# One kernel for attention and two MoE blocks: the last product takes hi and lo of its weight in one matmul, its pages come in the order of use, and early scores run on pieces of the array

## The chip, the core and the metric

The kernel runs on one core of one Trainium2 chip. The metric is the device time of one execution in microseconds (us). The kernel before was run three times: 1394.1, 1395.72 and 1396.98 us, median 1395.72. Its profiled execution took 1396.56 us, with a span of 1394.8 us from the first to the last instruction; 1.76 us lie around the span. The granted TensorE clock was 0.991 of full speed on average.

## The reference

Three stages, all in float32 outside (the weights come as float64 words and are converted on the chip):

```
# attention, 8 batches, 8 heads, 512 tokens x, 32 states, 64 columns a head
a  = softmax(x @ state.T / 8);  xread = a  @ state
a2 = softmax(state @ x.T / 8);  sread = a2 @ x
x  = concat(xread, sread)                     # 8 * 544 = 4352 rows of 512
x  = relu(x @ w_in) ** 2 @ w_out              # moe,  512 -> 2048 -> 512
h  = x @ w3                                   # moe2, 512 -> 2048
out = (h * sigmoid(h)) @ w4                   # moe2, 2048 -> 512
```

## The kernel before

**Precision.** TensorE works on two rounded parts. A float32 page of 128 partitions x 1024 is split into `hi` (a rounded copy made by ScalarE, `split_into`, line 457) and `lo` (the rest, a subtraction on VectorE or GpSimd). A product x times w is then three matmuls: hi.hi, hi.lo, lo.hi, all accumulated in one PSUM bank.

**Stages in order of time.** (1) 0 to some 50 us: the float64 words of the first weights are converted on VectorE and ScalarE, `g_unit` multiplies states by the first weight on 64x64 pieces of the array (four at once, plain float32), and the scores of batches 0 to 2 are made. (2) Up to some 850 us: the first MoE block, `gemm1`, `chain_a`, `gemm2`. (3) Some 850 to 1030 us: `gemm3`, the first product of the second block, in Strassen-Winograd form: 7 products of half matrices (numbers 1 to 7) whose sums give the four quarters. Its results go to DRAM as `t`. (4) Some 1030 to 1390 us: `gemm4(q)`, the second product in the same form, q = 0 to 8 (q = 8 has half the rows). The products come in the order 1, 6, 2, 7, 5, 4, 3 (`SEQ4`).

**gemm4.** Each product i of a q needs two half pages from DRAM, `g<q><i>0` and `g<q><i>1` (0.5 MB each), each split into hi and lo, so four pages; and four weight pages `w4<jj>_<i>`, which stay for all q, 28 in all, split when q is 0. A weight page holds for each of two row blocks 256 columns of hi and, right beside them, 256 columns of lo. The loop at lines 1051 to 1059 runs, for both halves b of the rows and 8 blocks k, three matmuls of 256 columns. Both b go into one PSUM bank of 512 columns; the four names bA to bD stand for banks that alternate with q. ScalarE copies the first product out (`u`), VectorE adds the others from PSUM into `u` or `z`, and `z[1]` (after product 4) and `z[0]` (after product 3, the last) are stored.

**What sets the order.** Nothing is ordered by hand: `Plan` records every operation with its tiles, and a list scheduler with estimated costs (`cost`, line 107) and due times writes each engine's queue. All pages come from one pool of 50; a load can be issued once its page is free. All DMAs are issued from one queue, SP's, in order. TensorE's queue often alternates between two products.

**Transition.** In the last unit of `gemm3` (u = 4), `w4_load(pp)` brings all seven pages of column block jj = pp before `gemm3(u, pp)`, for pp = 0 to 3. The pages of product 1 are therefore complete only with pp = 3.

**Scores of batches 0 to 2.** For each batch b and half g, `scores` (line 648) runs two float32 matmuls on the whole array: the stationary side is `sblkf[b]`, a 128x512 tile that is zero but for blocks of the states (set by `memset` on GpSimd, filled by `s_put`). The result psD is copied (`Sc`) and transposed by VectorE (`U`); from it the softmax on VectorE gives `AThi` and `ATlo`, on which `gemm1` starts.

Of the kernel before, what the change touches and what calls it, by code (L numbers as in the profile page):

```python
# [27 lines left out]
class Plan:  # L28
# [78 lines left out]
    def cost(self, eng, method, writes, reads, args):  # L107
        size = 1
        for ap in writes + reads:
            n = 1  # L110
            for d in ap.shape[1:]:
                n *= d
            size = max(size, n)
        psum = any(self.tiles.get(ap.tensor.name, (0, 0, ""))[2] == "ps" for ap in writes + reads)
        if eng == "dma":
            n = 1
            for d in writes[0].shape:
                n *= d
            return n * 4 / 360
        if eng == "pe":  # L120
            n = 1
            for d in writes[0].shape[1:]:
                n *= d
            if method == "transpose":
                return 109
            share = 4 if args.get("tile_position") else 1
            return max(n / 2.4 + 13, 109) * (4 if args["rhs"].dtype == F32 else 1) / share
        if eng == "act":
            return (145 if psum else 190) + size / 1.2 + (93 if "accum_out" in args else 0)
        if eng == "pool":  # L130
            return 190 + dict(tensor_tensor=2.2, memset=0.8).get(method, 3.5) * size
        fast = method in ("tensor_scalar", "tensor_copy", "memset") and not psum
        return 157 + size / (1.92 if fast else 0.96)
# [243 lines left out]
def attn_moe_moe_kernel(  # L377
# [76 lines left out]
    def copy(o, a):  # L454
        plan.either((A, "copy", dict(out=o, in_=a)), (V, "tensor_copy", dict(out=o, in_=a)))
# [101 lines left out]

    st = plan.tile(pages, [P, 4, 4, 2, NS], F32, "page", "st")
    sblk = [page(f"sblk{i}") for i in range(2)]
    sblkf = [quad(f"sblkf{b}") for b in range(NB)]  # L560
    ident = plan.tile(const, [P, P], F32, "ident", "ident")
    srT = plan.tile(pages, [P, 4, B * NS], F32, "page", "srT")

    def st_of(b, r):
        return st[r * 64:(r + 1) * 64, b // 2, :, b % 2].rearrange("p (g l) n -> p g l n", l=2)

    def s_build(b, dst, a):

        v = dst.rearrange("p (s g a c) -> p s g a c", s=2, g=2, a=4)
        for r in range(2):  # L570
# [1 line left out]
            src = st_of(b, r)  # L572
            hi, lo = (v[ps, s][:, :, a, r * NS:(r + 1) * NS] for s in range(2))
            split_into(hi, lo, src)

    def s_put(b, dst, a):

        v = dst.rearrange("p (g a c) -> p g a c", g=2, a=4)
        for r in range(2):
            ps = slice(r * 64, (r + 1) * 64)  # L580
            copy(v[ps, :, a, r * NS:(r + 1) * NS], st_of(b, r))


    w1p, gp = {}, {}
# [63 lines left out]
    def scores(b, g):  # L648
        x = a_x.pop((b, g))
        t = att_tile()  # L650
        a_S[(b, g)] = t
        if b < NB:
            for l in range(2):
                c0 = (2 * g + l) * P
                T.matmul(out=t, lhsT=sblkf[b][:, c0:c0 + P], rhs=x[:, l * 512:(l + 1) * 512],
                         start=l == 0, stop=l == 1)
            return
        hi, lo = x
        pg = sblk[b % 2]
# [265 lines left out]
    def w4_views(pg):  # L925
        v = pg.rearrange("p (k s c) -> p s k c", s=2, k=2)
        return v[:, 0], v[:, 1]

    def w4_load(jj):

        w4p[jj] = {}
        for i in SEQ4:
            w4p[jj][i] = page(f"w4{jj}_{i}")
            lo = f32(w4_views(w4p[jj][i])[1])
            if SRC_B[i] in (11, 12, 21, 22):
                w4_quarter(jj, SRC_B[i], lo)
            else:
                D.dma_start(lo, w4s_d[(SRC_B[i], jj)].rearrange("p (k c) -> p k c", k=2))

    def w4_split(jj, i):  # L940
        hi, lo = w4_views(w4p[jj][i])
        split_into(hi, lo, f32(lo))

    def x_op(u, i):
# [96 lines left out]

    def gemm4(q):

        c = 2 if q < B else 1
        n = c * 256

        def prod(i, bank, first, last):
            if q == 0:
                for jj in range(4):
                    w4_split(jj, i)  # L1050
            for b in range(c):
                for k in range(8):
                    hi, lo = gop[(q, i)][k // 4]
                    w = w4p[k // 2][i][:, k % 2 * 512:(k % 2 + 1) * 512]
                    ks = slice(k % 4 * c * P + b * P, k % 4 * c * P + (b + 1) * P)
                    for m, (g, o) in enumerate(((hi, 0), (hi, 256), (lo, 0))):
                        T.matmul(out=bank[:, b * 256:(b + 1) * 256], lhsT=g[:, ks], rhs=w[:, o:o + 256],
                                 start=first and b + k + m == 0, stop=last and k == 7 and m == 2,
                                 skip_group_check=True)

        def part(t):
            return t[:, :n].rearrange("p (b d) -> p b d", b=c)

        def add(o, bank, a):
            V.tensor_tensor(out=o, in0=part(bank), in1=a, op=ALU.add)
# [10 lines left out]
        bA, bB, bC, bD = (t[q % 2] for t in (BA, BB, BC, BD))  # L1076
        z = [page(f"z{t}", F32)[:, :c * 512].rearrange("p (b d) -> p b d", b=c) for t in range(2)]
        ls, hs = slice(0, 256), slice(256, 512)
        prod(1, bA, True, False)
        u = page("u4", F32)  # L1080
        U, W = (part(u[:, i * 512:(i + 1) * 512]) for i in range(2))
        A.copy(U, part(bA))
        prod(6, bB, True, True)
        add(U, bB, U)
        prod(2, bA, False, True)
        A.copy(z[0][:, :, ls], part(bA))
        prod(7, bD, True, False)
        add(W, bD, U)
        prod(5, bC, True, False)
        add(z[1][:, :, hs], bC, W)  # L1090
        prod(4, bD, False, True)
        add(z[1][:, :, ls], bD, U)
        store(1, z[1])
        prod(3, bC, False, True)
        add(z[0][:, :, hs], bC, U)
        store(0, z[0])


# [2 lines left out]
    def sched_attention(b, g, s, defer=False):  # L1101
        at(s - 4, "dma", x_load, b, g)
        if b >= NB:
            if g == 0:
                at(s, "vec", sblk_build, b)
            at(s, "vec", x_split, b, g)
        elif g == 0:
            at(s, "vec", s_put, b, sblkf[b], slice(0, 4, 3))
# [15 lines left out]
        at(s + 2, "vec", sread_evac, b, g)  # L1124

    def init():
        for t in sblkf:
            G.memset(t, 0.0)
        for t in sblk[::-1]:
            G.memset(t.bitcast(F32), 0.0)  # L1130

# [13 lines left out]
    for i in range(NC // 2):  # L1145
# [11 lines left out]
            at(-12, "dma", load_st)  # L1157
        at(n, "pe", g_unit, 2 * i)
        at(n, "pe", g_unit, 2 * i + 1)
    at(-10, "vec", s_put, 0, sblkf[0], slice(0, 4, 3))  # L1160
    for g in range(2):
        at(-8 + g, "dma", x_load, 0, g)
        at(-6 + g, "pe", scores, 0, g)
# [75 lines left out]
    for u in range(NU):  # L1239
        for pp in range(4):  # L1240
            plan.slot = base + 16 * u + 4 * pp
            if u == 0 and pp in (0, 1):
                w3_build(pp + 2)
            if u == 1:
                w4_sums(pp)
            if u + 1 == NU:
                if pp == 3:
                    g_op(0, 1)
                w4_load(pp)
            gemm3(u, pp)  # L1250
            if pp == 3:
                for i in (SEQ if u + 1 < NU else SEQ4[1:]):
                    if u + 1 < NU:
                        x_op(u + 1, i)
                    else:
                        g_op(0, i)
# [42 lines left out]
```

## Time and profile before

| what | value |
|---|---|
| median of three runs | 1395.72 us |
| profiled execution | 1396.56 us |
| its span | 1394.8 us |
| PE busy | 1350.0 us (97%) |
| VectorE (DVE) busy | 1006.7 us (72%) |
| ScalarE (ACT) busy | 693.0 us (50%) |
| GpSimd (POOL) busy | 44.8 us |
| DMA | 283 MB, mean 203 GB/s |

PE is TensorE's matmuls, PEld its weight loads, which run beside them. "PEclk" is the granted clock as a share of 2.4 GHz; the other level is 0.50. "DMA share" is the mean busy share of the core's 16 DMA engines. A float32 matmul that is not rounded shows as two instructions. In the rows below, `<-` after an idle time names what ended it.

### The profile page before, as it was taken

How to read it: one execution, taken by the hardware profiler on the slowest of the kernel's cores; microseconds unless marked ns; L12 is line 12 of the kernel's file. 1: busy time of each engine (PE TensorE's matmuls, PEld its weight loads, DVE VectorE, ACT ScalarE, POOL GpSimd, SP SyncE). 2: the span in 40 equal slices, each digit the busy share in tenths (PEclk: the TensorE clock that was granted, in tenths of full speed). 3: DMA queues.
4: the chain of work that ended last, by engine and by line, in shares of the span. 5: the costliest groups of instructions: out<-in, count | busy, mean ns of one | idle time of the engine just before them, and what ended most of it. 6: DMA issues, size and time to landing. Idle time of an engine off the chain costs nothing. (4 is left out here: it accounts for less than half of the span.)

```text
span 1394.8 us, 21037 instructions
## 1 busy us (share of the span) xinstructions
PE 1350.0 (97%) x7820; PEld 1169.2 (84%) x7820; DVE 1006.7 (72%) x1524; ACT 693.0 (50%) x1070; POOL 44.8 (3%) x42
## 2 busy tenths in 40 slices
PE   5889999999999999999999999999999999999998
PEld 1557688888888888888988889998879999999998
DVE  7898598878888888885997768677876455444443
ACT  6765776556555555554743424245563343333331
POOL 1000001100000000000020000000010000000000
PEclk9999999999999999999999999999999999999999
DMA  8841844535454535452759758678897566655664
GB/s 308 313 178 63 296 155 129 165 122 166 152 168 125 176 118 162 138 191 73 256 190 355 276 209 285 216 242 295 303 345 242 197 212 227 209 178 188 196 189 113
DMA packets 206965, 283.19 MB, mean 203 GB/s; under 512 B 13456, under 2 KB 148112, under 8 KB 206864
## 3 DMA queue, kind: packets, MB, share of 16 engines
q1 hardware_dynamic: 206864, 281.86, 60.7%
q8 instruction: 61, 1.00, 0.3%
q14 instruction: 40, 0.33, 0.1%
HBM read 161.35 MB, written 116.26 MB: 199 GB/s over the span
## 5 line engine op out<-in xcount | busy, mean ns | idle before, releaser
L185 ACT ACTIVATE rg<-psC 128x512 f32<-128x512 f32 (+1 forms) x144 | 82.6, 574 | 197.4 <-PE psC L185 195.4
L185 DVE TENSOR_TENSOR gact<-rg,gact 128x512 fp32r<-128x512 f32 (+1 forms) x139 | 90.8, 655 | 20.4 <-ACT rg L185 14.6
L185 PE MATMUL psC<-AThi,Ghi 128*128 128x512 f32 x256 | 100.9, 400 | 2.3 <-ACT rg L185 2.0
L185 PE MATMUL psC<-AThi,Glo 128*128 128x512 f32 x256 | 101.2, 401 | 1.6 <-DVE Glo L185 1.6
L185 PE MATMUL psC<-ATlo,Ghi 128*128 128x512 f32 x256 | 100.5, 397 | 1.9 <-DVE ATlo L185 1.9
L185 ACT ACTIVATE gact<-rg 128x512 fp32r<-128x512 f32 (+1 forms) x144 | 87.7, 609 | 7.6 <-DMA g<-go 4.1
L185 DVE TENSOR_TENSOR rg<-rg 128x512 f32<-128x512 f32 (+1 forms) x66 | 43.7, 662 | 50.5 <-ACT rg L185 50.3
L185 PEld LDWEIGHTS psC<-AThi,Ghi 128*128 128x128 f32 x256 | 48.1, 188 | 15.7 <-ACT rg L185 2.4
L185 PEld LDWEIGHTS psC<-AThi,Glo 128*128 128x128 f32 x256 | 48.2, 188 | 14.6 <-issue 2.1
L185 PEld LDWEIGHTS psC<-ATlo,Ghi 128*128 128x128 f32 x256 | 48.3, 189 | 13.8 <-DVE ATlo L185 2.6
L185 ACT ACTIVATE r<-r 128x1024 f32<-128x1024 f32 (+2 forms) x20 | 18.6, 932 | 62.9 <-DVE r L185 52.7
L185 DVE TENSOR_SCALAR cv<-cv 128x1024 f32<-128x1024 f32 (+1 forms) x64 | 43.3, 685 | 8.0 <-ACT cv L185 7.7
L185 ACT ACTIVATE rg<-rg 128x512 f32<-128x512 f32 (+1 forms) x78 | 46.3, 594 | 0.0
L185 ACT ACTIVATE cv<-raw 128x512 f32<-128x512 f32 x64 | 40.6, 667 | 7.3 <-DMA raw<-in_w_dram 6.3
L185 DVE SCALAR_TENSOR_TENSOR cc<-raw,cv 128x512 int32<-128x512 int32 x64 | 41.8, 683 | 3.3 <-DMA g<-go 3.1
L185 DVE SCALAR_TENSOR_TENSOR cv<-raw,cv 128x512 f32<-128x512 uint32 x64 | 41.6, 683 | 0.2
L185 DVE TENSOR_TENSOR W<-psC,U 128x512 f32<-128x512 f32 (+2 forms) x40 | 24.1, 609 | 22.5 <-PE psC L185 22.2
L185 PE MATMUL psA<-cc,st 64*64 64x512 f32 x128 | 26.1, 687 | 14.6 <-DVE cc L185 14.6
L185 DVE TENSOR_TENSOR Glo<-Glo,Ghi 128x1024 fp32r<-128x1024 f32 x31 | 37.7, 1215 | 1.2 <-ACT Ghi L185 1.0
L185 ACT ACTIVATE W<-W 128x1024 f32<-128x1024 f32 (+2 forms) x20 | 18.7, 933 | 39.6 <-DVE W L185 35.7
L185 ACT ACTIVATE r<-psA 128x512 f32<-128x512 f32 (+2 forms) x40 | 20.7, 534 | 33.3 <-PE psA L185 25.6
L185 ACT CAST Ghi<-Glo 128x1024 fp32r<-128x1024 f32 x32 | 33.5, 1045 | 1.2 <-DMA Glo<-go 1.2
(1244 smaller groups left out, 4587.2 us busy)
## 6 DMA issues: line engine op xcount, KB each, us to landing
raw<-in_w_dram SPq DMA_DIRECT2D x64, 512.0 KB, 6.2
t<-s SPq DMA_DIRECT2D x36, 512.0 KB, 5.1
Glo<-g SPq DMA_DIRECT2D x96, 128.0 KB, 4.3
t<-r SPq DMA_DIRECT2D x24, 512.0 KB, 4.5
xTr<-in_xT_dram SPq DMA_DIRECT2D x16, 512.0 KB, 7.6
g<-go SPq DMA_DIRECT2D x16, 512.0 KB, 5.2
xnr<-in_xN_dram SPq DMA_DIRECT2D x16, 512.0 KB, 5.2
x<-yt SPq DMA_DIRECT2D x32, 256.0 KB, 4.1
```

The source lines that it names most:

```text
L185: lambda engine=engine, method=method, a=a, k=k: getattr(engine, method)(*a, **k)))
```

## The change

Three edits.

1. `gemm4`: for each half b and block k there are two matmuls in place of three. hi.(hi and lo) is one matmul of 512 columns (the weight's hi and lo lie side by side), lo.hi one of 256 columns into the first half of the same bank. Each half b has a bank of its own (BA[0], BA[1], ...), so the banks no longer alternate with q. The two halves of a bank are now summed outside: every evacuation takes 512 columns for each b into pages of its own (`U4`, `R4`, `W4`, `X4`), and a `join` on VectorE or GpSimd adds the halves into `z`.
2. `w4_load(i, jj)` brings one page; the 28 come in the order of `SEQ4`, four for each product, seven after each `gemm3(u, pp)`.
3. `scores` for batches 0 to 2: four float32 matmuls on pieces of 64 rows x 32 columns, straight from `st`; `sblkf`, its memsets and `s_put` go. The planner's cost of a matmul on pieces goes by the size of the piece.

```diff
         if b < NB:
             for l in range(2):
-                c0 = (2 * g + l) * P
-                T.matmul(out=t, lhsT=sblkf[b][:, c0:c0 + P], rhs=x[:, l * 512:(l + 1) * 512],
-                         start=l == 0, stop=l == 1)
+                for r in range(2):
+                    h, ps = 2 * l + r, slice(r * 64, (r + 1) * 64)
+                    T.matmul(out=t[h * NS:(h + 1) * NS], lhsT=st[ps, b // 2, 2 * g + l, b % 2],
+                             rhs=x[ps, l * 512:(l + 1) * 512], start=True, stop=True, tile_position=(r * 64, h * NS))
...
-                    for m, (g, o) in enumerate(((hi, 0), (hi, 256), (lo, 0))):
-                        T.matmul(out=bank[:, b * 256:(b + 1) * 256], lhsT=g[:, ks], rhs=w[:, o:o + 256],
-                                 start=first and b + k + m == 0, stop=last and k == 7 and m == 2,
-                                 skip_group_check=True)
...
+                    T.matmul(out=banks[b], lhsT=hi[:, ks], rhs=w,
+                             start=first and k == 0, stop=False, skip_group_check=True)
+                    T.matmul(out=banks[b][:, 0:256], lhsT=lo[:, ks], rhs=w[:, 0:256],
+                             start=False, stop=last and k == 7, skip_group_check=True)
+
+        def new(name):
+            return page(name, F32)[:, :c * 512].rearrange("p (b n) -> p b n", b=c)
+
+        def add(o, banks, a):
+            for b in range(c):
+                V.tensor_tensor(out=o[:, b], in0=banks[b], in1=a[:, b], op=ALU.add)
+
+        def join(z, a):
+            arith(ALU.add, z, a[:, :, 0:256], a[:, :, 256:512])
...
+        prod(4, BD, False, True)
+        X = new("X4")
+        add(X, BD, U)
+        join(z[1][:, :, ls], X)
         store(1, z[1])
-        prod(3, bC, False, True)
-        add(z[0][:, :, hs], bC, U)
+        prod(3, BC, False, True)
+        add(U, BC, U)
+        join(z[0][:, :, hs], U)
         store(0, z[0])
...
-                w4_load(pp)
-            gemm3(u, pp)
+            gemm3(u, pp)
             if u + 1 == NU:
+                for i, jj in [(i, jj) for i in SEQ4 for jj in range(4)][7 * pp:7 * pp + 7]:
+                    w4_load(i, jj)
```

**TensorE in gemm4.** Where product 6 of q = 4 runs beside product 1; psA and psB are banks, w_1 and w_6 weight pages, g410 and g460 half pages of the stationary side (hi or lo). Before:

```order
L185 MATMUL psB_216<-w_6_1309,g460hi 128x256
L185 MATMUL psA_214<-w_1_1308,g410lo 128x256
L185 MATMUL psB_216<-w_6_1309,g460hi 128x256
L185 MATMUL psA_214<-w_1_1322,g410hi 128x256
L185 MATMUL psB_216<-w_6_1309,g460lo 128x256
L185 MATMUL psA_214<-w_1_1322,g410hi 128x256
L185 MATMUL psB_216<-w_6_1309,g460hi 128x256
```

Now:

```order
L186 MATMUL psB_216<-w_6_1316,g460hi 128x512
L186 MATMUL psA_215<-w_1_1312,g410lo 128x256
L186 MATMUL psB_216<-w_6_1316,g460lo 128x256
L186 MATMUL psA_215<-w_1_1313,g410hi 128x512
L186 MATMUL psB_216<-w_6_1316,g460hi 128x512
L186 MATMUL psA_215<-w_1_1313,g410lo 128x256
L186 MATMUL psB_216<-w_6_1316,g460lo 128x256
```

All matmuls were alike; now two long ones alternate with two short ones, and the two halves b (psA_214, psA_215) stand in banks of their own.

**VectorE in the transition.** The last sums of `gemm3` (s_ pages, stored to t) between the splits of g. With what each waits for: DVE, PE and Activation are engines, DMAHW a landing. Before:

```order
L185 TENSOR_TENSOR g020lo<-g020lo,g020hi 128x1024 [waits DMAHW1_49,Activation_49]
L185 TENSOR_TENSOR W<-r_1362,W 128x1024 [waits DVE_49]
L185 TENSOR_TENSOR s_1366<-s_1365,r_1362 128x1024 [waits PE_49]
L185 TENSOR_TENSOR g021lo<-g021lo,g021hi 128x1024 [waits DMAHW2_49,Activation_49]
L185 TENSOR_TENSOR s_1367<-U,s_1366 128x1024 [waits DMAHW0_49,DVE_49]
L185 TENSOR_TENSOR g070lo<-g070lo,g070hi 128x1024 [waits DMAHW4_49,Activation_49]
```

Now:

```order
L186 TENSOR_TENSOR W<-r_1352,W 128x1024 [waits DVE_49]
L186 TENSOR_TENSOR s_1356<-s_1355,r_1352 128x1024 [waits DMAHW0_49]
L186 TENSOR_TENSOR g020lo<-g020lo,g020hi 128x1024 [waits DMAHW1_49,Activation_49]
L186 TENSOR_TENSOR s_1357<-U,s_1356 128x1024 [waits DVE_49,PE_49,Activation_49]
L186 TENSOR_TENSOR g021lo<-g021lo,g021hi 128x1024 [waits DMAHW2_49,Activation_49]
L186 TENSOR_TENSOR g070lo<-g070lo,g070hi 128x1024 [waits DMAHW4_49,Activation_49]
```

The last sum, which stands ahead of the split of g070, took its page from a store that had to land; now it takes one from engines. The sum before it waits for a landing instead.

**SP's queue at the end of q = 3.** z is stored, g are the loads for q = 4. Before:

```order
L185 DMA out_dram<-z_1486 128x2x512
L185 DMA g450lo<-t_195 128x4x256
L185 DMA g451lo<-t_195 128x4x256
L185 DMA g440lo<-t_190 128x4x256
L185 DMA out_dram<-z_1485 128x2x512
L185 DMA g441lo<-t_190 128x4x256
L185 DMA g430lo<-t_185 128x4x256
L185 DMA g431lo<-t_185 128x4x256
```

Now:

```order
L186 DMA out_dram<-z_1492 128x2x512
L186 DMA g450lo<-t_195 128x4x256
L186 DMA g451lo<-t_195 128x4x256
L186 DMA g440lo<-t_190 128x4x256
L186 DMA g441lo<-t_190 128x4x256
L186 DMA out_dram<-z_1491 128x2x512
L186 DMA g430lo<-t_185 128x4x256
L186 DMA g431lo<-t_185 128x4x256
```

One load, g441, has moved ahead of the store of z[0]; g430 still stands behind that store.

## Rows read from the trace of the kernel before

**Rows 1.** Stretches of 50 us: length, busy us (instructions) by engine, PEclk, DMA share, GB/s

```profile
0.00:50.00 50.00, 32.38 (x156) 10.67 (x156) 38.11 (x61) 34.07 (x63) 3.88 (x11) 0.97 0.86 307
...
1000.00:1050.00 50.00, 44.16 (x239) 37.92 (x238) 39.25 (x48) 28.03 (x36) 4.75 (x3) 0.97 1.02 351
1050.00:1100.00 50.00, 50.00 (x402) 49.82 (x402) 27.79 (x27) 19.41 (x21) 0.00 (x0) 0.96 0.69 232
...
1150.00:1200.00 50.00, 49.79 (x415) 49.59 (x415) 24.34 (x23) 17.71 (x19) 0.00 (x0) 1.00 0.60 197
1200.00:1250.00 50.00, 47.96 (x388) 47.76 (x387) 22.60 (x23) 17.64 (x18) 0.00 (x0) 0.97 0.61 199
```

**Rows 2.** Waits of PE, 1050 us to the end: total us, times, longest

```profile
PE psA L185 <- ACT u L185: 4.7, 5, 2.0
```

**Rows 3.** Instructions in time (start us, us): DVE, SP, ACT, PE at q = 3's end

```profile
1207.40 0.68 DVE L185 TENSOR_TENSOR z<-psC,u 128x512 f32<-128x512 f32 x1
...
1208.15 0.38 SPq L185 DMA_DIRECT2D out_dram<-z  x1
1208.58 0.58 SPq L185 DMA_DIRECT2D g441lo<-t  x1
1209.25 1.30 SPq L185 DMA_DIRECT2D g430lo<-t  x1
...
1218.59 1.04 ACT L185 CAST g430hi<-g430lo 128x1024 fp32r<-128x1024 f32 x1 [0.29 <-DMA g430lo<-t]
1219.54 0.58 ACT L185 COPY u<-psA 128x512 f32<-128x512 f32 x1
...
1220.17 0.39 PE L185 MATMUL psA<-w,g420hi 128*128 128x256 f32 x1 [2.04 <-ACT u L185]
```

**Rows 4.** Waits of PE, 850 to 1060 us

```profile
PE psD L185 <- DVE g070lo L185: 3.5, 1, 3.5
PE psC L185 <- ACT g050hi L185: 1.7, 1, 1.7
...
PE psB L185 <- DMA t<-r: 0.6, 1, 0.6
```

**Rows 5.** Instructions in time: DVE around the last sum of gemm3

```profile
1046.47 1.23 DVE L185 TENSOR_TENSOR s<-U,s 128x1024 f32<-128x1024 f32 x1 [3.41 <-DMA t<-s]
1047.61 1.22 DVE L185 TENSOR_TENSOR g070lo<-g070lo,g070hi 128x1024 fp32r<-128x1024 f32 x1
```

**Rows 6.** Stretches at the start, columns as in Rows 1

```profile
28.00:32.00 4.00, 4.00 (x32) 1.20 (x26) 4.00 (x7) 3.69 (x8) 0.00 (x0) 1.00 0.48 140
...
88.00:92.00 4.00, 2.12 (x5) 1.10 (x6) 4.00 (x6) 0.00 (x0) 0.00 (x0) 0.51 0.00 0
92.00:96.00 4.00, 4.00 (x14) 3.21 (x13) 4.00 (x7) 1.76 (x3) 0.00 (x0) 0.64 0.00 0
```

**Rows 7.** Instructions in time: PE where 256-column matmuls of gemm4 meet 512-column ones

```profile
1026.93 0.28 PE L185 MATMUL psA<-w,g010hi 128*128 128x256 f32 x1
1027.05 0.40 PE L185 MATMUL psD<-x44hi,w 128*128 128x512 f32 x1
1027.28 0.28 PE L185 MATMUL psA<-w,g010hi 128*128 128x256 f32 x1
...
1027.99 0.40 PE L185 MATMUL psA<-w,g010hi 128*128 128x256 f32 x2
...
1029.41 1.07 PE L185 MATMUL psC<-x43hi,w 128*128 128x512 f32 x4
...
1030.77 0.39 PE L185 MATMUL psC<-x43hi,w 128*128 128x512 f32 x1
```

**Rows 8.** Instructions in time: PE at the start, scores (psD) between units on pieces

```profile
22.64 1.12 PE L185 MATMUL psD<-xTr,sblkf 128*128 128x512 f32 x2
23.70 1.09 PE L185 MATMUL psA<-cc,st 64*64 64x512 f32 x8
24.61 1.04 PE L185 MATMUL psB<-cc,st 64*64 64x512 f32 x8
25.57 1.12 PE L185 MATMUL psD<-xTr,sblkf 128*128 128x512 f32 x2
```

**Rows 9.** The end: DVE's last operation, from the chain of waits

```profile
1390.27 0.42 DVE z L185
```

More of the change, by code (lines that the diff above doesn't have):

```diff
@@ L125, in cost @@
                 return 109
-            share = 4 if args.get("tile_position") else 1
+            share = 128 * 128 // (reads[0].shape[0] * writes[0].shape[0]) if args.get("tile_position") else 1
             return max(n / 2.4 + 13, 109) * (4 if args["rhs"].dtype == F32 else 1) / share
@@ L559, in attn_moe_moe_kernel @@
     sblk = [page(f"sblk{i}") for i in range(2)]
-    sblkf = [quad(f"sblkf{b}") for b in range(NB)]
     ident = plan.tile(const, [P, P], F32, "ident", "ident")
@@ L574, in s_build @@
             split_into(hi, lo, src)
[L576 to L581, printed above, removed]
     w1p, gp = {}, {}
@@ L927, in w4_views, with w4_load @@
         return v[:, 0], v[:, 1]
[L929 to L938, printed above, removed]
+    def w4_load(i, jj):
+        w4p[(jj, i)] = page(f"w4{jj}_{i}")
+        lo = f32(w4_views(w4p[(jj, i)])[1])
+        if SRC_B[i] in (11, 12, 21, 22):
+            w4_quarter(jj, SRC_B[i], lo)
+        else:
+            D.dma_start(lo, w4s_d[(SRC_B[i], jj)].rearrange("p (k c) -> p k c", k=2))
     def w4_split(jj, i):
-        hi, lo = w4_views(w4p[jj][i])
+        hi, lo = w4_views(w4p[(jj, i)])
         split_into(hi, lo, f32(lo))
@@ L1044, in gemm4, with prod @@
         c = 2 if q < B else 1
-        n = c * 256
-        def prod(i, bank, first, last):
+        def prod(i, banks, first, last):
             if q == 0:
@@ L1053, in prod @@
                     hi, lo = gop[(q, i)][k // 4]
-                    w = w4p[k // 2][i][:, k % 2 * 512:(k % 2 + 1) * 512]
+                    w = w4p[(k // 2, i)][:, k % 2 * 512:(k % 2 + 1) * 512]
                     ks = slice(k % 4 * c * P + b * P, k % 4 * c * P + (b + 1) * P)
-                    for m, (g, o) in enumerate(((hi, 0), (hi, 256), (lo, 0))):
-                        T.matmul(out=bank[:, b * 256:(b + 1) * 256], lhsT=g[:, ks], rhs=w[:, o:o + 256],
-                                 start=first and b + k + m == 0, stop=last and k == 7 and m == 2,
-                                 skip_group_check=True)
[L1061 to L1065, printed above, removed]
+                    T.matmul(out=banks[b], lhsT=hi[:, ks], rhs=w,
[9 more added lines that the diff above has]
+            arith(ALU.add, z, a[:, :, 0:256], a[:, :, 256:512])
         def store(t, z):
@@ L1074, in store @@
                     D.dma_start(out[r0:r0 + NS, :], z[i * NS:(i + 1) * NS, 0, :])
-        bA, bB, bC, bD = (t[q % 2] for t in (BA, BB, BC, BD))
-        z = [page(f"z{t}", F32)[:, :c * 512].rearrange("p (b d) -> p b d", b=c) for t in range(2)]
+        z = [new(f"z{t}") for t in range(2)]
         ls, hs = slice(0, 256), slice(256, 512)
[L1079 to L1092, printed above, removed]
+        prod(1, BA, True, False)
+        U = new("U4")
+        for b in range(c):
+            A.copy(U[:, b], BA[b])
+        prod(6, BB, True, True)
+        add(U, BB, U)
+        prod(2, BA, False, True)
+        R = new("R4")
+        for b in range(c):
+            A.copy(R[:, b], BA[b])
+        join(z[0][:, :, ls], R)
+        prod(7, BD, True, False)
+        W = new("W4")
+        add(W, BD, U)
+        prod(5, BC, True, False)
+        add(W, BC, W)
+        join(z[1][:, :, hs], W)
+        prod(4, BD, False, True)
+        X = new("X4")
+        add(X, BD, U)
+        join(z[1][:, :, ls], X)
         store(1, z[1])
-        prod(3, bC, False, True)
-        add(z[0][:, :, hs], bC, U)
+        prod(3, BC, False, True)
+        add(U, BC, U)
+        join(z[0][:, :, hs], U)
         store(0, z[0])
@@ L1106, in sched_attention @@
             at(s, "vec", x_split, b, g)
-        elif g == 0:
-            at(s, "vec", s_put, b, sblkf[b], slice(0, 4, 3))
         at(s + 1, "pe", scores, b, g)
@@ L1126, in init @@
     def init():
-        for t in sblkf:
-            G.memset(t, 0.0)
         for t in sblk[::-1]:
@@ L1159, in attn_moe_moe_kernel @@
         at(n, "pe", g_unit, 2 * i + 1)
-    at(-10, "vec", s_put, 0, sblkf[0], slice(0, 4, 3))
     for g in range(2):
@@ L1245, in attn_moe_moe_kernel @@
                 w4_sums(pp)
+            if u + 1 == NU and pp == 3:
+                g_op(0, 1)
+            gemm3(u, pp)
             if u + 1 == NU:
-                if pp == 3:
-                    g_op(0, 1)
-                w4_load(pp)
-            gemm3(u, pp)
+                for i, jj in [(i, jj) for i in SEQ4 for jj in range(4)][7 * pp:7 * pp + 7]:
+                    w4_load(i, jj)
             if pp == 3:
```

## The prediction

> **What bounds the kernel now.** I read the stretches of 50 us first: from 150 us on PE is busy for nearly all of every stretch, at a granted clock of 1.00, so a change is worth what it takes from PE there, and only next what it takes from waits. Three places stand out [rows 1]: the start (PE 32.4 of 50 us), the passage from gemm3 to gemm4 (44.2 of 50, DMA share 1.02, clock 0.97 and then 0.96), and gemm4 itself, where one stretch has 48.0 of 50 and a clock of 0.97. In gemm4 the matmuls of 256 columns follow one another every 49.79 / 415 = 0.120 us [rows 1].
>
> The waits of PE come next. In gemm4 there is one kind: PE waits for the copy u, five times, 4.7 us in all, at most 2.0 [rows 2]. The instructions in time show why, at the end of q = 3 [rows 3]: the last add into z starts at 1207.40, the store of z goes out at 1208.15, the load of g430 behind it in SP's queue at 1209.25, and lands before 1218.6; ScalarE's queue has the rounding of g430 ahead of the copy u, and PE stands for 2.04 us until 1220.17. In the passage PE waits 3.5, 1.7 and 0.6 us [rows 4]. The longest is for the split of g070, which VectorE could not begin since the last sum of gemm3 stood in front of it and waited 3.41 us for a store of t to land [rows 5].
>
> At the start it is VectorE that sets the pace: it is busy 4.00 of 4 us at 28 to 32 us, and again at 88 to 96 us, where PE stands idle and falls to half clock [rows 6].
>
> **The change part by part.**
>
> *The matmul in gemm4.* For q = 0 to 7 there are 7 x 2 x 8 = 112 groups of three matmuls, for q = 8 there are 56: 952 groups, 0.360 us each. Each becomes one matmul of 512 columns and one of 256. The columns stay 768; what goes is a fixed part per matmul. Alone, 512-column matmuls follow one another in (1030.77 - 1029.41) / 6 = 0.227 us [rows 7], so 0.227 + 0.120 = 0.347 is the low end. Where the two lengths alternate one by one, three pairs take 1027.99 - 1026.93 = 1.06 us, 0.353 a pair [rows 7]. The new queue goes long, short, short, long, half as many changes, so I take 0.350 between the two: 952 x 0.010 = 9.5 us less. Ends: 952 x 0.013 = 12.4 less, and none, if the first stage of a long matmul costs what was saved. PE is the bound of this stage, so it counts in full.
>
> The page "TensorE: Matmul & The Clock Gate" of the Trainium skill (Back-to-back issue gap) gives N/2.4 + 2.5 ns for an isolated gap; by it three short matmuls take 328 ns, a pair 325 ns, and the edit saves some 2.5 us. The trace has 120 where the rule has 109 and 227 where it has 216, so here I go by the rows.
>
> *Evacuation and join.* VectorE gets, for each q, ten adds of 512 columns in place of five, and four joins: nine more at 0.68 us [rows 3], 6 us of some 39. Its splits of g take 14 x 1.22 [rows 5] = 17 us of each q, so it stays under 70%. Hidden beside PE, but for the end of a q, below. ScalarE gets two more copies of 0.58 [rows 3], hidden likewise. No bank is read late: each half of A, B, C and D is used again a product or more after its reader.
>
> *The end of a q.* The chain of [rows 3] gets one join, 0.68, between the last add and the store of z; the load of g441, 1209.25 - 1208.58 = 0.67 us of SP's queue, now stands ahead of that store. PE's own work from the end of q to its wait is 98 short matmuls before, 11.76 us; counted in the new queue with 0.227 and 0.120 it is 11.67. So three terms cancel and the wait stays: 0. Low end: no wait any more, -4.7, and the half clock after it, 3% of the stretch from 1200 [rows 1], -1.5. High end: pages. The pool has 50, 28 hold weights, and a q now holds up to six others in place of three; loads get fewer pages ahead. If each of eight ends waited as long as the worst did, 8 x (2.04 + 1.5) - 6.2 = +22.
>
> *The order of the weight pages.* The passage lost 3.5 + 1.7 + 0.6 = 5.8 us in waits [rows 4] and 1.5 + 2.0 in clock [rows 1], 9.3 in all. The new last sum of gemm3 waits for no landing, so the 3.41 us [rows 5] before the split of g070 go; product 5, whose half page was waited for 1.7 us, starts after product 2 in the new queue instead of before it; and then the clock need not fall. What is late next is the DMA: its share is 1.02 here [rows 1] and no byte goes, so part of the wait comes back on g060 or g070. I take 5 less; ends 9.3 less, and 0.
>
> *The scores.* A score of one b and g was two matmuls on the whole array, each 23.70 - 22.64 = 1.06 us (two instructions). Four pieces of 64x64 (eight instructions) take 24.61 - 23.70 = 0.91 to 25.57 - 24.61 = 0.96 [rows 8]. Four pieces of 64x32 I take the same: 6 x (2.12 - 0.94) = 7.1 us of PE less. Six small copies on ScalarE and three memsets go too. But VectorE holds the path here [rows 6], and nothing of its work goes, so I take 1 less. Ends: 7.1 less, and 3.4 more, if PE with less to do falls to half clock for another spell like the one at 88 to 96 us (4 x 0.49 + 4 x 0.36 [rows 6]).
>
> The page "TensorEngine Tiling (Array Packing)" of the Trainium skill (Gotcha 1: PSUM Pressure) says that different row tiles cannot access the same PSUM bank at once. By it the four pieces, which all write psD's bank, would go in two turns. The 64x64 pieces of [rows 8] come from both halves of the rows, write one bank too, and go in one turn, so the rows speak against it; by the rule the scores would save PE nothing.
>
> *The end of the kernel.* Behind the last matmul VectorE had 0.42 us [rows 9]; now an add and a join of at most 0.68 each [rows 3], +0.7, with no cover.
>
> Sum: 1396.56 - 9.5 + 0 - 5 - 1 + 0.7 = 1381.8, taken as 1381.5 us. The profiled execution is 0.84 us above the median of the three runs shown, well inside the ranges below.
>
> **The rivals.**
>
> *Slower: the ends of q.* Each z and each new sum takes a whole page, the load of g431 now stands behind the landing of a store of z, and in SP's single queue all later loads stand behind it. PE would then wait at most ends, and each wait of 2 us brings half clock: +22 from above, and the passage and the start give nothing: 1396.56 - 9.5 + 22 + 0.7 = 1409.8. It decides from 8.8 / 8 = 1.1 us more per end on. Against it: the loads stand in the same order, VectorE is free a third of the time, and only one wait in five was as long as 2 us.
>
> *Nothing from the merge.* A pair costs 0.360 like the three: 1381.5 + 9.5 = 1391, and if the passage stays bound by DMA as well, 1396. For it: in [rows 7] a long matmul after a short one starts later than after a long one.
>
> *All waits go.* The pair costs 0.347, the passage gives 9.3, the ends 6.2 and the scores 7.1: 1396.56 - 12.4 - 9.3 - 6.2 - 7.1 + 0.7 = 1362. Against it: DMA and VectorE, as above.
>
> *Pieces in two turns.* The scores then take PE as long as before: 1381.5 + 1 = 1382.5, hardly to be told in the time, but in the rows. This is what the page on array packing would give.
>
> *The plan does not do what it says.* A new list may place things worse in the first block, where PE has no gap: a few us either way, inside the range.
>
> **How the numbers follow.** The forecast, 1372 to 1389 by its own bounds, gets 0.58, with 0.03 more for pieces in two turns; all waits go (1360 to 1372) 0.14; nothing from the merge 0.15, of which a third stays within 0.2%; slower 0.10. What a measurement can tell from no change is some 0.2%, 2.8 us. So faster 0.58 + 0.03 + 0.14 + 0.10 = 0.85, same 0.05, slower 0.10. The range for 8 in 10 leaves out the slower case and a part of the lowest: 1366 to 1394.
>
> **What would show it.** In the new profile: in gemm4 pairs every 0.350 us, stages of q 0.010 x 112 = 1.1 us shorter (PE without waits); four score pieces in 0.94 us, the first gemm1 matmul no more than 1 us earlier; no wait on the split of g070 of 3 us, and clock 1.00 from 1050; still a wait at the copies U of some q, 5 us in all. I would be wrong if PE waits in gemm4 sum to over 12 us, if a pair costs 0.360, or if DMA-bound waits on g move from one product to the next.

## The result

The changed kernel takes 1382.58 us, the median of 4 runs (1379.83 to 1383.69); before, timed beside it, 1394.91 us (1393.72 to 1396.98). The ratio is 0.9899, 95% interval 0.9882 to 0.9916: 12.3 us faster by the medians, 14 by the ratio (interval 12 to 16). The profiled execution has a span of 1380.1 us, against 1394.8 us.

The stretches of 50 us of the changed kernel, with the columns of [rows 1]:

```profile
0.00:50.00 50.00, 30.47 (x169) 8.61 (x170) 35.76 (x58) 30.82 (x54) 2.48 (x8) 1.00 0.75 259
...
950.00:1000.00 50.00, 48.61 (x238) 40.65 (x238) 39.70 (x55) 26.41 (x39) 5.02 (x3) 1.00 0.89 294
1000.00:1050.00 50.00, 48.31 (x228) 39.91 (x227) 45.28 (x53) 29.77 (x42) 7.07 (x4) 1.00 1.01 352
1050.00:1100.00 50.00, 47.52 (x269) 40.60 (x269) 34.49 (x37) 22.57 (x26) 2.38 (x1) 1.00 0.74 250
1100.00:1150.00 50.00, 50.00 (x288) 43.47 (x288) 33.08 (x37) 22.14 (x24) 0.00 (x0) 1.00 0.65 211
```

Read the last one first. 288 matmuls, 144 pairs, in 50.00 us are 0.347 us a pair, where three short ones took 0.360 [rows 1]. Then the clock: it is 1.00 in all of them, where before had 0.97 and 0.96. Then the idle time of PE: 1.7 us in the passage (1000 to 1050 us) in place of 5.8, but 1.4 us ahead of it and 2.5 us behind it, where before lost nothing.

Where long and short matmuls follow one another, PE shows the pairs one by one (start, duration):

```profile
1080.78 0.40 PE L186 MATMUL psA<-w,g110hi 128*128 128x512 f32 x1
1081.01 0.40 PE L186 MATMUL psA<-w,g111hi 128*128 128x512 f32 x1
1081.25 0.28 PE L186 MATMUL psA<-w,g110lo 128*128 128x256 f32 x1
1081.37 0.27 PE L186 MATMUL psA<-w,g111lo 128*128 128x256 f32 x1
1081.48 0.40 PE L186 MATMUL psA<-w,g110hi 128*128 128x512 f32 x1
```

Two pairs from 1080.78 to 1081.48 are 0.70 us. Each start lies 0.23 to 0.24 us behind a long matmul and 0.11 to 0.12 behind a short one: the alternation costs next to nothing. (The count of a stretch takes in both its edges. From start to start a pair takes 0.349 us, and three short ones in before 0.363; the difference is 0.013 to 0.014 either way.)

PE's waits in the changed kernel, from 850 to 1060 us and from 1050 us to the end (us in all, times, longest), against [rows 4] and [rows 2]:

```profile
PE psA L186 <- ACT U L186: 1.7, 3, 0.9
PE psD L186 <- ACT g070hi L186: 0.9, 1, 0.9
PE psD L186 <- DVE g070lo L186: 0.5, 1, 0.5
PE psD L186 <- DVE W L186: 0.2, 1, 0.2
...
PE psD L186 <- DVE W L186: 1.9, 2, 1.3
PE psA L186 <- ACT U L186: 1.9, 4, 0.8
```

The 3.5 us on g070lo are 0.5. The waits at the copies of U, 4.7 us before, are 1.9, none longer than 0.8, and no half clock follows. A wait on W has come in that was not there.

The start went the other way. From 150 to 650 us PE has no gap in either kernel, so one matmul behind that stretch tells what the start cost; of before, then of the changed kernel:

```profile
648.01 0.28 PE L185 MATMUL psC<-srhi,w1s0hi 128*128 128x256 f32 x1
```

```profile
652.25 0.28 PE L186 MATMUL psC<-srhi,w1s0hi 128*128 128x256 f32 x1
```

So the start lost 4.2 us in this execution. The last add and its join, the end that answers to [rows 9], of the changed kernel:

```profile
1374.46 0.69 DVE L186 TENSOR_TENSOR U<-psC,U 128x512 f32<-128x512 f32 x1 [0.35 <-PE psC L186]
1375.18 0.42 DVE L186 TENSOR_TENSOR z<-U 128x256 f32<-128x256 f32 x1
```

They take 1.14 us where 0.42 stood, 0.7 more.

| term | forecast | read from the two profiles |
|---|---|---|
| merged matmul | -9.5 | 952 x (0.360 - 0.3472) = -12.2 |
| ends of q | 0 | waits 4.7 to 1.9, half clock 1.5 to 0: -4.3 |
| passage | -5 | waits 5.8 + clock 3.5 to 3.3 + 1.9: -4.1 |
| scores and start | -1 | +4.2 |
| end | +0.7 | +0.7 |
| sum | -14.8 | -15.7 (the spans differ by 14.7) |

The rows do not close to better than some 2 us. Before has 0.9 us of waits more between 850 and 1060 us than the 5.8 counted here, and 0.3 us of the waits on U lie in both stretches of the changed kernel; with these two put right, the rows sum to -16.9.

The forecast was right within 1.1 us of the median. Two of its terms were not, and their errors cancel: that the sum came out so close is luck.

### The profile page after: what moved, and what is told of

It reads as the page before. It is cut to its first block, busy times and chain, and to the rows that moved or that the text cites. A ratio compares the mean times of both kernels' runs of the same rounds, so it can differ in the third digit from the quotient of the medians.

```text
span 1380.1 us, 19261 instructions
## 1 busy us (share of the span) xinstructions
PE 1335.8 (97%) x6892; PEld 1107.9 (80%) x6892; DVE 1056.3 (77%) x1598; ACT 701.0 (51%) x1080; POOL 48.9 (4%) x41
## 5 line engine op out<-in xcount | busy, mean ns | idle before, releaser
L186 DVE TENSOR_TENSOR W<-psD,U 128x512 f32<-128x512 f32 (+2 forms) x57 | 35.4, 631 | 35.9 <-PE psD L186 35.8
L186 PEld LDWEIGHTS psC<-AThi,Glo 128*128 128x128 f32 x256 | 48.0, 188 | 16.2 <-issue 3.3
L186 PEld LDWEIGHTS psC<-ATlo,Ghi 128*128 128x128 f32 x256 | 48.2, 189 | 14.8 <-DVE ATlo L186 2.9
L186 DVE TENSOR_TENSOR U<-psB,U 128x512 f32<-128x512 f32 (+2 forms) x57 | 35.0, 629 | 14.1 <-PE psB L186 12.6
L186 ACT COPY U<-psA 128x512 f32<-128x512 f32 (+2 forms) x57 | 28.9, 538 | 14.9 <-PE psA L186 14.3
```

The lines of the kernel that those rows point to most:

```text
L186: lambda engine=engine, method=method, a=a, k=k: getattr(engine, method)(*a, **k)))
```

## The experiments

The change has three edits that touch different stretches: with the scores alone the order of instructions differs from before's in the first block only, with either of the other two only from gemm3's last unit on. So they can be had one by one. Times are medians; before took 1396.1 to 1396.5 us beside these runs. A difference from before in us comes from the ratio, times 1396, and one between two of the kernels from their medians, unless said otherwise.

**One edit alone, and two of them.**

Scores alone, with the planner's new charge for a piece (gemm4 and the weight pages as before):

```
-                T.matmul(out=t, lhsT=sblkf[b][:, c0:c0 + P], rhs=x[:, l * 512:(l + 1) * 512],
-                         start=l == 0, stop=l == 1)
+                for r in range(2):
...
+                    T.matmul(out=t[h * NS:(h + 1) * NS], lhsT=st[ps, b // 2, 2 * g + l, b % 2],
...
```

> Before with the scores on pieces (and the planner's share) alone. Theory A, from the rows of the changed kernel: the list of the first block comes out in another order, VectorE's first copy go waits 2.7 us longer, and all that follows starts 4.2 us later: 4 us slower than before (+3 to +5), first matmul of gemm2 4.2 us later, no change after it. Rival B, the term of the prediction: the scores are worth 1 us (up to 7 us) less time, and the late start of the changed kernel comes from the other two edits.

Measured: 1401.6 us, ratio 1.0047 (1.0030 to 1.0063), 6.6 us slower (interval 4 to 9), so theory A's place, and more than its 3 to 5. The matmul on w1s0hi starts at 652.43 us, 4.4 us later than in before, and from there to the end this execution takes as long as before's (746.4 and 746.8 us). This edit is what makes the start late.

The change without the scores on pieces, and with before's charge (against the changed kernel):

```
-                for r in range(2):
...
-                    T.matmul(out=t[h * NS:(h + 1) * NS], lhsT=st[ps, b // 2, 2 * g + l, b % 2],
...
+                T.matmul(out=t, lhsT=sblkf[b][:, c0:c0 + P], rhs=x[:, l * 512:(l + 1) * 512],
+                         start=l == 0, stop=l == 1)
```

> The change without the scores on pieces: the merged matmul in gemm4 and the order of the weight pages. Theory A: the first block is that of before, so the start's 4.2 us come back: 16 us faster than before (-14.5 to -18), 4 us faster than the changed kernel. Rival B: 13 us faster than before, no faster than the changed kernel, since the scores cost nothing.

Measured: 1381.67 us, ratio 0.9893 (0.9878 to 0.9908), 15 us faster than before, 1 us from the changed kernel. The time does not tell the theories apart. The place does: the matmul on w1s0hi starts at 648.77, 3.5 us sooner than in the changed kernel, as theory A has it. But PE lost 1.5 us between 650 and 770 us in this execution, where the changed kernel's lost 0.1. Executions differ by as much: in a second profile of the changed kernel, below, that matmul starts at 654.68, 2.4 us later than in its first.

Merge alone:

```
-        for m, (g, o) in enumerate(((hi, 0), (hi, 256), (lo, 0))):
-            T.matmul(out=bank[:, b * 256:(b + 1) * 256], lhsT=g[:, ks], rhs=w[:, o:o + 256],
...
+        T.matmul(out=banks[b], lhsT=hi[:, ks], rhs=w,
...
+        T.matmul(out=banks[b][:, 0:256], lhsT=lo[:, ks], rhs=w[:, 0:256],
...
```

> Before with the merged matmul of gemm4, its banks and joins alone. Theory A: three short matmuls cost 0.361 us with all that lies between, a long and a short one 0.349 us, which is 952 x 0.012 = 11.4 us; and the waits at the ends of q go here too (4.7 us and 1.7 us of half clock), since the extra pages hold back the load of g of product 3's second half, and so the load that PE waits for lands 3 us sooner: 15 to 17 us faster with the tail's 1 us against it. Rival B: the end waits go because the weight pages come in another order; then this edit alone is 10 to 11 us faster and PE still waits some 5 us at the copies U. Rival C: the prediction's 0.350 and no change at the ends, 9 us faster.

Measured: 1379.15 us, ratio 0.9866 (0.9846 to 0.9887), 18.7 us faster by the ratio and 17.1 by the medians; the same kernel once more, below, 16.2 and 17.4. Theory A, near its upper end, though not all the waits at the copies U go (3.0 us of 4.7 are left, in the repeat 2.4). It is faster than the whole change.

Order of the weight pages alone:

```
-                w4_load(pp)
-            gemm3(u, pp)
+            gemm3(u, pp)
+                for i, jj in [(i, jj) for i in SEQ4 for jj in range(4)][7 * pp:7 * pp + 7]:
+                    w4_load(i, jj)
```

> Before with the new order of the weight pages alone. Theory A: the waits in the passage from gemm3 to gemm4 and the half clock behind them go for the most part: 3 to 5 us faster, and the waits at the ends of q stay at about 5 us in all. Rival B: without the merged matmul the passage gives nothing, since the DMA is full there: within 1 us of before. Rival C: it gives all of the passage's waits and the ends' too, 9 to 14 us faster.

Measured: 1390.24 us, ratio 0.9954 (0.9940 to 0.9969), 6.4 us faster. Theory A has the direction and not all of the size. PE's waits from 850 to 1060 us are these:

```profile
PE psA L185 <- ACT U L185: 0.9, 1, 0.9
PE psD L185 <- DVE W L185: 0.3, 1, 0.3
```

That is 1.2 us in all, where before's waits in [rows 4] make 5.8: this edit alone clears the passage.

Merge and scores, pages as before (against the changed kernel):

```
+                w4_load(pp)
             gemm3(u, pp)
...
-                for i, jj in [(i, jj) for i in SEQ4 for jj in range(4)][7 * pp:7 * pp + 7]:
-                    w4_load(i, jj)
```

> The changed kernel with the weight pages in before's order (merge and scores alone). Theory A: the merge alone already takes most of the waits in the passage, and the new order of the pages gives nothing on top: 0 to 3 us faster than the changed kernel. Rival B: the order of the pages is worth 6 us here as it was alone: 1387 to 1390 us.

Measured: 1384.45 us, ratio 0.9913 (0.9893 to 0.9932). It is 2 us slower than the changed kernel by the medians, not up to 3 faster as theory A had it, and the intervals overlap; rival B, 1387 to 1390, falls.

Scores and pages' order, gemm4 as before (against the changed kernel):

```
-                    T.matmul(out=banks[b], lhsT=hi[:, ks], rhs=w,
...
+            for m, (g, o) in enumerate(((hi, 0), (hi, 256), (lo, 0))):
...
```

> The changed kernel with gemm4 as before (scores on pieces and the order of the weight pages alone). Theory A: the parts measured alone, 6 us slower and 6 us faster, add up: within 2 us of before. Rival B: the scores cost only 1 us where the pages come in the new order, as the difference of the changed kernel and the one without the scores says: 4 to 6 us faster than before.

Measured: 1393.95 us, ratio 0.9988 (0.9971 to 1.0005). Theory A: 6.6 slower and 6.4 faster add up.

What follows from the six: without the merge the order of the pages is worth 6.4 and, with scores, 8.3 us; with the merge it is worth between 1 and 4 us slower (the change without scores against the two runs of merge alone, by the ratios) and 2 us faster (the change against merge and scores). The profiles say the same without the start. One matmul divides each of them, the first on w1s0hi:

| kernel | its start, us | from there to the end, us |
|---|---|---|
| before | 648.0 | 746.8 |
| scores | 652.4 | 746.4 |
| pages' order | 648.4 | 738.5 |
| scores and pages' order | 653.4 | 737.4 |
| merge, two profiles | 647.2, 648.3 | 729.9, 728.4 |
| merge and pages' order | 648.8 | 731.9 |
| merge and scores | 652.2 | 730.7 |
| the change, two profiles | 652.3, 654.7 | 727.8, 728.8 |

The scores move the start alone, and behind it the order of the pages is worth 8 to 9 us without the merge and nothing clear with it. The two edits take the same wait. The last sum of gemm3 waited for the landing of a store [rows 5]; in merge alone (first) and in pages' order alone (second) it does not:

```profile
1041.99 1.22 DVE L185 TENSOR_TENSOR s<-U,s 128x1024 f32<-128x1024 f32 x1 [0.21 <-ACT U L185]
```

```profile
1043.37 1.22 DVE L185 TENSOR_TENSOR s<-U,s 128x1024 f32<-128x1024 f32 x1
```

It is gone in each kernel that has one of these edits, and stays, 3.2 us or more, where neither is made (in scores alone 3.22). What in the merge's list removes it was not separated. Merge alone keeps another wait, 3.5 us for g050 (2.3 in the repeat), and a clock of 0.97 from 1000 to 1050 us. With both edits there is instead a new chain, which both profiles of the changed kernel show. Here from the first, VectorE, ScalarE, GpSimd and PE in time:

```profile
1057.10 1.05 ACT L186 CAST g040hi<-g040lo 128x1024 fp32r<-128x1024 f32 x1 [5.61 <-DMA t<-s]
...
1058.17 1.23 DVE L186 TENSOR_TENSOR g040lo<-g040lo,g040hi 128x1024 fp32r<-128x1024 f32 x1 [5.13 <-ACT g040hi L186]
...
1064.21 0.69 DVE L186 TENSOR_TENSOR W<-psD,U 128x512 f32<-128x512 f32 x1
1064.65 2.38 POOL L186 TENSOR_TENSOR g110lo<-g110lo,g110hi 128x1024 fp32r<-128x1024 f32 x1 [23.70 <-ACT g110hi L186]
1064.81 2.78 DVE L186 TENSOR_TENSOR z<-R 128x512 f32<-128x512 f32 x1
...
1067.51 0.68 DVE L186 TENSOR_TENSOR W<-psD,U 128x512 f32<-128x512 f32 x1
...
1068.24 0.50 PE L186 MATMUL psD<-w,g040hi 128*128 128x512 f32 x1 [1.32 <-DVE W L186]
```

The rounding of g040 waits 5.6 us for a transfer, VectorE stands behind it, and its sums W come late; between the two halves of W stands a join that takes 2.78 us beside GpSimd's split and ends 0.56 us behind it. Product 4 writes the bank that W is read from, so PE waits 0.6 and 1.3 us.

**What in the merge gives the gain.** Merge alone, but the long matmul in its two halves again; banks, joins and pages stay:

```
-                    T.matmul(out=banks[b], lhsT=hi[:, ks], rhs=w,
...
+                    T.matmul(out=banks[b][:, 0:256], lhsT=hi[:, ks], rhs=w[:, 0:256],
...
+                    T.matmul(out=banks[b][:, 256:512], lhsT=hi[:, ks], rhs=w[:, 256:512],
...
```

> The merge-only kernel (banks, joins and pages of the changed gemm4), but hi times hi and lo again as two matmuls of 256 columns: three short matmuls into the new banks. Theory A: the gain of the merge-only kernel is 11 to 12 us from the length of the queue and 5 to 6 us from shorter waits; this one keeps the waits' part: 4 to 7 us faster than before. Rival B: the gain is the matmul's alone, and the joins and pages cost a little: 0 to 3 us slower than before. Rival C: the banks give it all (no bank of 512 columns is shared by two b any more): 15 us or more faster.

Measured: 1391.2 us, ratio 0.9962 (0.9945 to 0.9979), 5.3 us faster than before and 12 us slower than merge alone. Theory A. A stretch of 50 us of this kernel, and of merge alone:

```profile
1250.00:1300.00 50.00, 49.92 (x415) 49.65 (x414) 31.21 (x34) 20.52 (x23) 0.00 (x0) 1.00 0.56 179
```

```profile
1250.00:1300.00 50.00, 50.00 (x289) 43.62 (x288) 30.75 (x34) 21.07 (x23) 0.00 (x0) 1.00 0.66 211
```

49.92 / 415 x 3 = 0.361 us for three short ones, 50.00 / 289 x 2 = 0.346 for a pair. The matmul is worth 12 us, the rest of the edit 5 us. The profile of this kernel shows where the rest may lie: its last sum of gemm3 waits for no store either, PE's waits from 850 to 1060 us are 3.0 us in place of 6.7, the clock from 1000 to 1100 us is 1.00, and the waits at the copies U are 3.3 us in place of 4.7.

To see where those 5 us come from, before with three more pages taken in each q, for as long as R4, W4 and X4 live:

```
         add(W, bD, U)
+        R = page("W4", F32)
+        V.tensor_copy(out=R[:, 0:8], in_=W[:, 0, 0:8])
...
+        V.tensor_copy(out=R[:, 8:16], in_=z[1][:, 0, 256:264])
```

> Before, with three more pages of the pool taken in each q of gemm4 for as long as the changed kernel's R4, W4 and X4 live (VectorE writes 8 columns of each, twice), and nothing else. Theory A: the part of the gain that stayed in the kernel of three short matmuls (5 us) comes from pages that are free later, which holds back loads of g and lets the one that PE waits for land sooner: 3 to 6 us faster than before, the wait in the passage under 3 us. Rival B: the pages give nothing or cost loads their head start, as the prediction's slower rival says: 0 to 10 us slower; then the 5 us come from the separate banks and copies.

Measured: 1392.36 us, ratio 0.9976 (0.9963 to 0.9989), 3.4 us faster. More pages taken do not make the kernel slower, so rival B falls, but theory A does not stand as it was put. The last sum of gemm3 waits as long as before, and PE's waits in gemm4 (whose list here is no longer quite before's) are shorter:

```profile
1048.08 1.22 DVE L185 TENSOR_TENSOR s<-U,s 128x1024 f32<-128x1024 f32 x1 [4.32 <-DMA t<-s]
```

```profile
PE psA L185 <- ACT u L185: 2.6, 5, 1.2
```

From the issue of the load of product 3's first half to its rounding 7.7 to 9.6 us pass for q = 1 to 7, against 8.1 to 9.3 in before: the load does not land sooner, so the mechanism is not the one I gave. In the changed kernel it does. SP and ScalarE at the same place as [rows 3]:

```profile
1202.17 0.36 SPq L186 DMA_DIRECT2D g441lo<-t  x1
1202.62 0.46 SPq L186 DMA_DIRECT2D out_dram<-z  x1
1203.17 0.42 SPq L186 DMA_DIRECT2D g430lo<-t  x1
1208.37 0.36 SPq L186 DMA_DIRECT2D g431lo<-t  x1
...
1209.70 1.05 ACT L186 CAST g430hi<-g430lo 128x1024 fp32r<-128x1024 f32 x1 [1.57 <-DMA g430lo<-t]
1210.66 1.07 ACT L186 COPY U<-psA 128x512 f32<-128x512 f32 x2
```

6.5 us after its issue g430 is rounded; it was 9.3 [rows 3]. For q = 2 to 7 the time is 6.1 to 7.4 us here; for q = 1 it is 9.8. The load of g431, which stands behind z's landing, goes out 5.2 us after g430's. In before it followed 1.6 us behind g430's (1209.25 [rows 3]):

```profile
1210.85 1.36 SPq L185 DMA_DIRECT2D g431lo<-t  x1
```

So the late load of g431, which the prediction's slower rival feared, goes with a sooner g430. That it is the reason is not shown. The loads ahead are less crowded too: g441, which stands in front of both, is rounded 4.9 us after its issue (1202.17 to 1207.08), where before's took 8.7 (1208.58 to 1217.25). And in merge alone g130 is rounded 6.4 us after its issue with g131 only 0.6 us behind it. How much of the ends' 4.3 us this is stays open as well: scores alone, whose gemm4 has before's list, shows 7.2 us at the copies of u, where before shows 4.7, so one profile of an end is good to some 2.5 us. Over all profiles from 1050 us on, these waits are 3.7 to 7.2 us in the four kernels with before's gemm4 and 1.9 to 3.9 in those with the merged matmul.

**Why the scores cost the start.** VectorE, in the changed kernel, and PE ahead of it:

```profile
19.77 1.90 PE L186 MATMUL psD<-xTr,st 64*32 64x512 f32 x10
21.60 1.07 PE L186 MATMUL psB<-cc,st 64*64 64x512 f32 x4
22.61 1.04 PE L186 MATMUL psD<-xTr,st 64*32 64x512 f32 x2
23.58 1.08 PE L186 MATMUL psB<-cc,st 64*64 64x512 f32 x4
24.59 1.05 PE L186 MATMUL psD<-xTr,st 64*32 64x512 f32 x4
25.56 1.09 PE L186 MATMUL psA<-cc,st 64*64 64x512 f32 x8
26.47 1.04 PE L186 MATMUL psB<-cc,st 64*64 64x512 f32 x8
```

```profile
27.61 0.69 DVE L186 COPY go<-psB 128x512 f32<-128x512 f32 x1 [5.66 <-PE psB L186]
```

A piece is two instructions, so x10 is five pieces and x8 four. Pieces that start together make one turn, and a turn takes 0.86 to 1.01 us here, whether it holds four pieces or one. The four pieces of a score can go in one turn: those of the last score all start between 79.89 and 79.92 us, and the first four pieces here between 19.77 and 19.79. But the list tears scores apart: of the next four pieces one starts at 20.65, one at 22.61 and two at 24.59, in three turns, with four pieces of a unit cut into two halves between them. These are six turns from 19.77 us on, so psA's pieces, which stand at 23.70 in before [rows 8], start at 25.56, and VectorE's copy of go stands until 27.61. So it goes on: the 24 pieces of the six scores take 12 turns, only three of them with four pieces, and before had 12 whole matmuls. In before VectorE's copy is this:

```profile
24.95 0.69 DVE L185 COPY go<-psA 128x512 f32<-128x512 f32 x1 [3.21 <-PE psA L185]
```

The planner charges a piece of 64x32 half of a piece of 64x64 (share 8 against 4), 0.45 us for a score that takes 0.9 us or more. So: the change with the full charge for every piece.

```
-            share = 128 * 128 // (reads[0].shape[0] * writes[0].shape[0]) if args.get("tile_position") else 1
+            share = 4 if args.get("tile_position") else 1
```

> The changed kernel, with the planner charging every piece as it does 64x64 pieces (share 4), so a piece of 64x32 is charged double: the list of the first block alternates one score with one pair of units again, as before's does. Theory A (the order of the list costs the start its 4 us, the pieces themselves cost nothing): VectorE's first copy go waits some 3.2 us again in place of 5.7, gemm2 starts 4 to 6 us sooner, and the kernel is 4 us faster than the changed one (1376 to 1380 us). Rival B (the pieces themselves, or the copies and memsets that went, cost the start): the start stays as late as in the changed kernel, within 1.5 us of its time.

Measured: 1381.76 us, ratio 0.9900 (0.9881 to 0.9918): no faster than the changed kernel, so theory A's time fails, though its place holds. The copy of go waits 3.01 us again, and the first matmul of gemm1 comes 4.8 us sooner than in the changed kernel (at 48.01) and 2 us sooner than in before (45.20):

```profile
43.23 0.74 PE L186 MATMUL psC<-AThi,Ghi 128*128 128x512 f32 x2
...
70.94 0.74 PE L186 MATMUL psA<-gact,hi('w2', 1)_306 128*128 128x512 f32 x2 [3.94 <-DVE gact L186]
```

Then it is lost: from 64 to 68 us VectorE does nothing, the DMA is full, and at w1s0hi (650.63) 1.6 of the 4.8 us are left.

```profile
64.00:68.00 4.00, 2.99 (x14) 2.10 (x12) 0.00 (x0) 0.41 (x1) 0.00 (x0) 1.00 1.02 370
```

The change once more, and merge alone once more, side by side (kernels as above, no edit):

> The changed kernel once more, beside the merge-only kernel. Theory A: its start is again 4 us later than before's and the merge-only kernel is 3 us faster. Rival B: the two are within 1 us, and the 3 us were a difference of the runs.

> The merge-only kernel once more, beside the changed one. Theory A: 1378 to 1380 us, 3 us under the changed kernel. Rival B: 1381 to 1383 us.

Measured: 1381.56 us, ratio 0.9906 (0.9888 to 0.9924), and 1379.05 us, ratio 0.9884 (0.9863 to 0.9906). Merge alone is again 2.5 us under the change. The intervals overlap, but of the nine executions of the change only two lie under the slowest of the eight of merge alone (1380.57), so rival B is unlikely. The start of the change is late again, and by more: w1s0hi at 654.68 us.

Merge and scores, with the planner charging a score what it charged for before's two whole matmuls:

```
+            share = 4 if args.get("tile_position") else 1
+            if share == 4 and writes[0].shape[0] == 32:
+                share = 2
```

> Merge and scores on pieces, the weight pages in before's order, and the planner charging a score what before's two whole matmuls were charged (twice the charge of the kernel with share 4). Theory A: the time of the start hangs on the list that comes out, not on the pieces: the first matmul of gemm1 starts before 48.0 us, where the changed kernel has it, and the kernel lies 1 to 5 us under the merge and scores kernel (1384.5 us). Rival B: pieces cost the start 4 us in any list: within 1 us of it.

Measured: 1377.99 us, ratio 0.9873 (0.9855 to 0.9890), 6.5 us under merge and scores with the change's charge. Theory A, though by a little more than it had. The same pieces in another list, 11 turns for the six scores, and the start is as early as in before:

```profile
45.51 0.73 PE L188 MATMUL psC<-AThi,Ghi 128*128 128x512 f32 x2
...
647.37 0.28 PE L188 MATMUL psC<-srhi,w1s0hi 128*128 128x256 f32 x1
```

It has the lowest median of all, but only 1 us under merge alone, which is within the noise: with this charge the pieces cost nothing, and that they gain something is not shown. This charge together with the new order of the pages was not run.

## Why the prediction was right in sum and wrong in two terms

*The merged matmul: right, the size at its low end.* I took 0.350 us a pair, between 0.347 and 0.353, for a queue that changes between long and short half as often. It costs 0.346 to 0.347 by the same count that gave 0.360 for three. The term is 12.2 us by the rows and 12 us by the run that splits the matmul again, not 9.5. The 0.353 of [rows 7] for a changing queue at gemm3's end was too dear for gemm4. The Trainium skill's "TensorE: Matmul & The Clock Gate" (Back-to-back issue gap) has a rule for an isolated gap, and by it I estimated 2.5 us for this term; the runs have 12.

*The ends of q: the sum of three cancelling terms was wrong.* I had the wait stay, with -6.2 as the low end; it fell by 4.3 us, half clock included. What failed is that I left the landing of g's load as it was: the load that PE waits for is rounded 2.8 us sooner after its issue at the end of q = 3, and 1 to 3 us sooner for the loads of q = 2 to 7. The runs show this place, not why it lands sooner, nor how much of the 4.3 us hangs on it.

*The passage: right, and for half of the reason.* The wait of the last sum of gemm3 went, as forecast, and the clock stayed at 1.00. That "part of the wait comes back on g060 or g070" was the right kind: 1.4 us came back on g070, and 1.9 us on W behind g040, which I had not named. What I did not see is that the merge alone takes the 3.4 us wait too. So this edit adds nothing that these runs can tell where the merge is made (728 to 732 us behind w1s0hi with it and without it).

*The scores: wrong in sign, and outside its range.* The step that failed is "VectorE holds the path here [rows 6], and nothing of its work goes, so I take 1 less", with 3.4 more as the worst end. The 7.1 us of PE are not there either: I took the four pieces of a score as one turn, and the list spreads them over two on average. That is the count of the rival of two turns, but not for the bank's sake: all four pieces of the last score start within 0.03 us of each other at 79.89 us. (In [rows 8] psA names two banks with two pieces in each, so those rows showed less than I read from them: two pieces to a bank, not four.) And the change to the planner's charge reorders the first block, and VectorE's in-order queue waits 5.66 us where it waited 3.21. All five profiles of kernels with this charge have the start 4 to 7 us later than before's; the six others with before's scores lie within 1.4 us of it. Merge and scores take 6.5 us less with nothing but the charge changed. I had this as the rival "The plan does not do what it says", with "a few us either way, inside the range", and gave it no chance of its own and no term in the sum.

*The end: right*, 0.7 us with no cover.

Of the signs that I named for being wrong, one came: DMA-bound waits did move from one product's g to another's, from g070 to g040. At 3.3 us it did not decide.

## What to carry to other kernels

A sum that comes out right shows little about its terms: edits that touch different stretches can be taken apart by the order alone and timed one by one. Where a list scheduler sets the order, a change to its charges is an edit of its own, and the queue that waits in order is where it is paid. Two edits that remove the same wait must not both be credited with it.

## What the runs showed of the hardware that was not expected

- Long and short matmuls in turn take together what one of each takes alone (0.227 and 0.120 us): 0.23 us behind 512 columns, 0.11 to 0.12 behind 256, so 0.347 a pair, where three of 256 take 0.360.
- A turn of float32 pieces of 512 columns took 0.86 to 1.01 us at the start of the changed kernel, with four pieces of 64x64 or 64x32, with two, or with one alone.
- A VectorE join of 128x512, 0.69 us elsewhere, took 2.78 us while GpSimd ran a split of 128x1024 for 2.4 us, in both profiles of the changed kernel, and ended 0.54 to 0.56 us behind it. The change without the scores and the change with share 4 show the same (2.77 us).
- A load of 512 KB landed and was rounded 9.3 us after its issue with the next load 1.6 us behind it, and 6.5 us after with the next load 5.2 us behind. The gap is not shown to be the cause: another landed and was rounded in 6.4 us with the next load 0.6 us behind it.
